# Moving columns of both layers' products taken in turn from two halves of the operand

## The chip, the cores and the metric

The kernel runs on 1 core of one Trainium2 chip. The metric is the device time of one execution in microseconds, as the median of several runs. One more execution is taken with a profiler; durations and rows below come from that one.

## The reference

Pooled attention feeds a two-layer block with a rational activation. Everything is float32. Cut to what matters:

```python
# q, k, v: (8, 8, 576, 64); pool = 8 keys or values are averaged into one
attn = softmax(q @ mean8(k).T / 8)            # 72 pooled keys per head
x = (attn @ mean8(v)) -> (4608, 512)          # tokens x (heads * head_dim)
h = x @ w_in                                  # (4608, 2048)
P = a[0] + a[1]*h + a[2]*h*h + a[3]*h*h*h
Q = 1 + abs(b[0])*abs(h) + abs(b[1])*h*h
out = (P / (Q + 1e-6)) @ w_out                # (4608, 512)
```

## The kernel before

**Blocks.** The 4608 tokens are worked in 18 blocks of 256 (`TOK`), the 2048 inner columns in 8 units of 256 (`NU`). For each block `attend` (line 860) makes the attention output, already transposed: 512 model columns on 4 x 128 partitions, 256 tokens along the free dimension. For each pair of block and unit there are three steps: `mm1` (line 925, first layer), `rational` (line 944, the activation on ScalarE, VectorE and GpSimd) and `mm2` (line 981, second layer).

**Split numbers.** The type fp32r keeps fewer bits of a float32. So each operand is kept as two fp32r parts, a high one and a low one, and each product is the sum of three: high by high, high by low, low by high. x is the pair of tiles `xs[0]`, `xs[1]` (128 x 4 x 256); a weight tile `w` has both parts, `w[:, 0, :]` and `w[:, 1, :]`.

**First layer.** `mm1` does 24 products for each block and unit into one PSUM bank `ph` (128 inner columns x 2 x 256 tokens). The stationary operand is 128 x 128 of `w_in`, the moving operand is `xs[xi][:, c, :]`: 256 consecutive tokens (line 938).

**Second layer.** `mm2` does 12 products for each block and unit into two banks `po` (128 tokens x 512 output columns, one for each half of the block). The stationary operand is 128 x 128 of the activation (`gh` or `gl`), the moving operand 512 consecutive columns of a row of `w_out` (line 991). The banks collect over the units; then `evict` (line 1024) scales and copies bank 0 on VectorE and bank 1 on ScalarE into `ob`, which is sent to `out`. Blocks 0 and 1 are done in two halves of the units: their first sum goes to memory and is fetched and added by `scalar_tensor_tensor` (line 1014).

**Where x is made.** `values` (line 826) multiplies the pooled values by the attention weights into a bank `pv` (2 x 256 tokens for two of the four groups of model columns), ScalarE copies it to `xs[0]` in fp32r (line 846) and VectorE subtracts that copy from `pv` into `xs[1]` (line 847). This happens twice in a block, for groups 0 and 1 and for groups 2 and 3.

**What sets the order.** Nothing is issued as it is written. Each operation is added to a `Plan` with a cost, a due time and what it reads and writes; `solve` (line 168) simulates the engines and picks the order of every engine, and `issue` (line 266, the calls on line 299) emits it. The costs are constants: 118.1 ns for a product of the first layer (line 935), 231.6 ns for one of the second (line 990). Between real products the plan puts filler products (line 290) where TensorE would stand idle: early ones multiply `identr` by itself with 256 moving columns, later ones add zeros, with one column of zeros repeated 256 times as the moving operand.

A dependency in the plan goes by `Lazy.box` (line 53): the region of a tile that an operand names. It is known only where the operand is cut by plain indices; with a `rearrange` it is empty, and an empty box meets every other one:

```python
            if name != "__getitem__":
                return ()
```

For the very first units of block 0, `mm1` splits its products into those of groups 0 and 1 and those of groups 2 and 3 (`parts`, line 930), so that the first can go ahead of the second half of x.

Of the kernel before, what the change touches and what calls it, by code (L numbers as in the profile page):

```python
# [8 lines left out]
F32 = mybir.dt.float32  # L9
# [3 lines left out]
ALU = mybir.AluOpType  # L13
# [9 lines left out]
class Lazy:  # L23
# [29 lines left out]
    def box(self):  # L53

        for name, args, _ in self.chain:
            if name == "bitcast":
                continue
            if name != "__getitem__":
                return ()
            idx = args[0] if isinstance(args[0], tuple) else (args[0],)  # L60
            out = []
            for i, n in zip(idx, self.tile.shape):
                out.append((i, i + 1) if isinstance(i, int) else
                           (i.start or 0, n if i.stop is None else i.stop))
            return tuple(out)
        return ()


def meet(a, b):
# [31 lines left out]
class Plan:  # L101
# [27 lines left out]
    def add(self, eng, cost, calls, port=False, claims=(), bytes=0, early=38, after=()):  # L129
# [5 lines left out]
        for _, args, kw in calls:  # L135
            every = list(args) + list(kw.values())
            dst = kw.get("out", args[0] if args else None)
            for v in every:
                if isinstance(v, Lazy) and v is not dst:
                    box = v.box()  # L140
                    op.deps.update(o for o, x in v.tile.writes if meet(x, box))
                    v.tile.reads.append((op, box))
                    touched[id(v.tile)] = v.tile
            if isinstance(dst, Lazy):
                t, box = dst.tile, dst.box()
                op.deps.update(o for o, x in t.writes if meet(x, box))
                op.deps.update(o for o, x in t.reads if meet(x, box))
                if box == ():
                    t.writes, t.reads = [], [r for r in t.reads if r[0] is op]
                t.writes.append((op, box))  # L150
                touched[id(t)] = t
# [167 lines left out]
def tile_pooled_attention_then_rational_moe(  # L319
# [18 lines left out]
    NT, DM = out.shape  # L338
    DFF = w_in.shape[1]
    P = 128  # L340
# [5 lines left out]
    TOK = 256  # L346
# [29 lines left out]
    def new(where, tag, shape, dtype, name):  # L376
        return plan.tile(*pools[where], shape, dtype, tag, name)

    def bank(name, shape):
        return new("ps", "ps", shape, F32, name)  # L380

    dve = Engine(plan, "dve", 0.09999999999999999, 1.04)
    act = Engine(plan, "act", 0.105, 0.85)
    gp = Engine(plan, "pool", 0.242, 2.021)

    def pe(ns, calls, claims=(), after=()):
        return plan.add("pe", ns / 1000, calls, claims=claims, after=after)

    def mm(out, lhsT, rhs, start, stop):
        return "matmul", (out,), dict(lhsT=lhsT, rhs=rhs, start=start, stop=stop)  # L390

    def dma(kbytes, dst, src, run=2048, issue=0.48, early=60.0, after=()):

        plan.add("sp", issue, [("dma_start", (dst, src), {})], early=early, after=after,
                 bytes=kbytes * 1024 * (1 + 312 / run))
# [52 lines left out]
    WS = 2.0 ** 8  # L448
# [220 lines left out]
    def segs(t0, n):  # L669

        r, t = [], t0
        while t < t0 + n:
            e = min(t0 + n, (t // S + 1) * S)
            r.append((t - t0, e - t0, t // S))
            t = e
        return r
# [149 lines left out]
    def values(i, hi, lo, before=None):  # L826

        xs = [new("xs", f"x{s}", [P, NJ, TOK], F32R, f"x{s}_{i}") for s in range(2)]
        for c in range(2):
            if before:  # L830
                before(c)
            pv = bank(f"pv{i}_{c}", [P, 2, TOK])
            calls = []
            for jj in range(2):
                j = 2 * c + jj
                for r0, r1, n in segs(i * TOK, TOK):
                    vh, vl = vm[n % 2]
                    o = pv[:, jj, r0:r1]
                    terms = ((o, vh[:, j, :], hi[:, j, r0:r1]), (o, vl[:, j, :], hi[:, j, r0:r1]),
                             (pv[:D, jj, r0:r1], vr[n % 2][:, j, :], lo[:, NJ + c, r0:r1]),  # L840
                             (o, vh[:, j, :], lo[:, j, r0:r1]))
                    calls += [mm(dst, vals, probs, s == 0, s == 3)
                              for s, (dst, vals, probs) in enumerate(terms)]
            pe(117.4 * 8 if len(calls) == 8 else 1635, calls, claims=xs)
            cs = slice(2 * c, 2 * c + 2)
            act(2 * TOK).copy(xs[0][:, cs, :], pv)
            dve(2 * TOK).tensor_tensor(
                out=xs[1][:, cs, :], in0=pv, in1=xs[0][:, cs, :].bitcast(F32),
                op=ALU.subtract)
        return xs  # L850

    prepared = set()
# [7 lines left out]
    def attend(i):  # L860
# [27 lines left out]
        if i >= SQ:  # L888

            for a in range(4):  # L890
# [15 lines left out]
            dve(2 * TOK, port=True).tensor_tensor(  # L906
                out=both[0], in0=both[1], in1=own, op=ALU.subtract)
        return values(i, hi, lo)


# [14 lines left out]
    def mm1(i, u, xs):  # L925
        ph = bank(f"ph{i}_{u}", [P, 2, TOK])
        n = DM // P
        w = weights["win", u]
        last = ()
        parts = [range(n)] if i or u > 1 else [range(n // 2), range(n // 2, n)]  # L930
        for h, cs in enumerate(parts):
            plan.now += 8 * h
            for f in range(2):
                for s, (wi, xi) in enumerate(((0, 0), (0, 1), (1, 0))):
                    last = pe(118.1 * len(cs), [
                        ("matmul", (ph[:, f, :],), dict(
                            lhsT=w[:, wi, (2 * c + f) * P:(2 * c + f + 1) * P],
                            rhs=xs[xi][:, c, :], start=f == 0 and s == 0 and c == 0,
                            stop=s == 2 and c == n - 1, skip_group_check=True))
                        for c in cs], after=last),  # L940
        plan.now -= 8 * h
        return ph
# [14 lines left out]
    def last(i, u):  # L957
        return i == NBLK - 1 and u == NU - 1
# [20 lines left out]
    pos, parts = {}, {}  # L979

    def mm2(i, u, gh, gl):
        u0, u1 = (0, NU) if i >= 2 else (0, NA) if u < NA else (NA, NU)
        if u == u0:
            pos[i] = [bank(f"po{i}_{u}_{m}", [P, DM]) for m in range(2)]
        w = weights["wout", u]
        terms = [(f, *x) for f in range(2) for x in ((gh, 0), (gh, 1), (gl, 0))]

        def products(n, ms):
            f, g, wi = terms[n]
            return pe(231.6 * len(ms), [  # L990
                mm(pos[i][m], g[:, f, m * P:(m + 1) * P], w[:, wi, f * DM:(f + 1) * DM],
                   u == u0 and n == 0, u == u1 - 1 and n == 5)
                for m in ms], claims=[pos[i][m] for m in ms])

        if last(i, u):
            for m in range(2):
                plan.now += 10.0 * m
                for n in range(6):
                    products(n, (m,))
                ob = new("dec", "m", [P, DM], F32, f"ob{i}_{m}")  # L1000
                evict(m, ob, pos[i][m])
                dma(256, out[i * TOK + m * P:i * TOK + (m + 1) * P, :], ob)
            return
        for n in range(6):
            end = products(n, (0, 1))
        if u < u1 - 1:
            return
        ob = new("dec", "m", [P, 2, DM], F32, f"ob{i}_{u}")
        if i < 2 and u0:
            dma(512, ob, parts.pop(i), after=(end,))  # L1010
        for m in range(2):
            po = pos[i][m]
            if i < 2 and u0:
                dve(DM).scalar_tensor_tensor(out=ob[:, m, :], in0=po, scalar=1.0 / WS,
                                             in1=ob[:, m, :], op0=ALU.mult, op1=ALU.add)
            else:
                evict(m, ob[:, m, :], po)
        if i < 2 and not u0:
            parts[i] = new("hbm", f"pd{i}", [P, 2, DM], F32, f"pd{i}")
            dma(512, parts[i], ob)  # L1020
        else:
            dma(512, out[i * TOK:(i + 1) * TOK, :].rearrange("(m p) x -> p m x", p=P), ob)

    def evict(m, dst, po):
        if m == 0:
            dve(DM).tensor_scalar(out=dst, in0=po, scalar1=1.0 / WS, scalar2=None, op0=ALU.mult)
        else:
            act(DM).activation(dst, po, AF.Copy, scale=1.0 / WS)
# [22 lines left out]
    xs, kept = {}, {}  # L1051
# [65 lines left out]
```

## Time and profile before

| | |
|---|---|
| median of 3 runs | 927.87 us (927.82 to 928.4) |
| the profiled execution's own time | 928.65 us |
| its span, from the first to the last instruction | 926.9 us |
| mean granted TensorE clock | 0.998 |
| busy: TensorE, VectorE, ScalarE, GpSimd | 99%, 82%, 73%, 57% of the span |

The profile's page lists the busy time of each engine, a chain of waits that is followed back from the last instruction, and groups of instructions. Nearly all instructions come from line 299, so groups are told apart by the names of their tiles. The length that a product has in such a row is the time it is in the pipeline, and consecutive products overlap; what a product costs in a stream is the time from its start to the next one's start. That is read from the chain or the timeline: the time of a stretch of one kind divided by its count, or the difference of two starts.

### The profile page before, as it was taken

How to read it: one execution, taken by the hardware profiler on the slowest of the kernel's cores; microseconds unless marked ns; L12 is line 12 of the kernel's file. 1: busy time of each engine (PE TensorE's matmuls, PEld its weight loads, DVE VectorE, ACT ScalarE, POOL GpSimd, SP SyncE). 2: the span in 40 equal slices, each digit the busy share in tenths (PEclk: the TensorE clock that was granted, in tenths of full speed). 3: DMA queues.
4: the chain of work that ended last, by engine and by line, in shares of the span. 5: the costliest groups of instructions: out<-in, count | busy, mean ns of one | idle time of the engine just before them, and what ended most of it. 6: DMA issues, size and time to landing. Idle time of an engine off the chain costs nothing.

```text
span 926.9 us, 17117 instructions
## 1 busy us (share of the span) xinstructions
PE 916.0 (99%) x6158; PEld 834.1 (90%) x6158; DVE 764.6 (82%) x1335; ACT 677.1 (73%) x1126; POOL 529.7 (57%) x474
## 2 busy tenths in 40 slices
PE   7999999999999999999999999999999999999998
PEld 7899999999998999999999899999999899999996
DVE  5989988798879888878888798879896988787764
ACT  2888888777677867776776877686867676777774
POOL 4787787685547644445644574457544755444452
PEclk9999999999999999999999999999999999999999
DMA  9995201163233412122603160215312231202000
GB/s 275 309 386 189 47 29 45 32 158 103 46 82 75 119 24 58 28 59 52 143 9 71 37 161 11 39 42 128 73 28 54 69 81 22 59 1 59 1 23 23
DMA packets 185072, 75.32 MB, mean 81 GB/s; under 512 B 162332, under 2 KB 162332, under 8 KB 184988
## 3 DMA queue, kind: packets, MB, share of 16 engines
q1 hardware_dynamic: 184988, 74.23, 31.1%
q8 instruction: 49, 0.80, 0.4%
q14 instruction: 35, 0.29, 0.1%
HBM read 50.59 MB, written 12.58 MB: 68 GB/s over the span
## 4 chain that ended last, share of the span: by engine, by line
PE 92%; DVE 2%; SPq 2%; ACT 1%; DMA 1%; issue 0%; POOL 0%; ACTq 0%
PE po L299 41%; PE ph L299 41%; PE pv L299 4%; PE ps L299 4%; SPq L299 2%; DMA q<-in_q_dram 1%; DVE t L299 1%; PE pvs L299 0%; PE pq L299 0%; DVE e L299 0%; DVE sm L299 0%; PE pk L299 0%; DVE am L299 0%; PE pm L299 0%; PE pvr L299 0%
## 5 line engine op out<-in xcount | busy, mean ns | idle before, releaser
L299 PEld LDWEIGHTS ph<-x,win 128*128 128x128 f32 x3264 | 480.1, 188 | 60.6 <-ACT x L299 0.9
L299 PE MATMUL ph<-x,win 128*128 128x256 f32 x3264 | 497.5, 279 | 0.8 <-ACT x L299 0.5
L299 PE MATMUL po<-wout,gh 128*128 128x512 f32 x1152 | 355.7, 395 | 0.0
L299 POOL TENSOR_TENSOR w<-w,r 128x512 f32<-128x512 f32 (+1 forms) x145 | 192.7, 1329 | 260.5 <-ACT r L299 257.4
L299 POOL TENSOR_TENSOR gl<-t,gh 128x512 fp32r<-128x512 f32 (+1 forms) x145 | 191.8, 1323 | 77.2 <-ACT gh L299 76.5
L299 PEld LDWEIGHTS po<-wout,gh 128*128 128x128 f32 x1152 | 179.7, 188 | 7.7 <-issue 0.4
L299 PE MATMUL po<-wout,gl 128*128 128x512 f32 x576 | 180.9, 395 | 0.0
L299 DVE SCALAR_TENSOR_TENSOR t<-t,abn,rp 128x512 f32<-128x512 f32 (+1 forms) x145 | 107.0, 739 | 50.2 <-ACT rp L299 48.5
L299 ACT ACTIVATE t<-ph,abn 128x512 f32<-128x512 f32 (+1 forms) x145 | 112.1, 773 | 34.9 <-PE ph L299 22.9
L299 DVE TENSOR_TENSOR t<-t,ph 128x512 f32<-128x512 f32 (+1 forms) x145 | 97.9, 676 | 37.4 <-ACT t L299 36.4
L299 ACT ACTIVATE r<-w,abn 128x512 f32<-128x512 f32 (+1 forms) x145 | 117.6, 811 | 13.4 <-POOL gl L299 6.8
L299 ACT ACTIVATE w<-ph 128x512 f32<-128x512 f32 (+1 forms) x145 | 86.1, 594 | 51.5 <-PE ph L299 31.2
L299 ACT CAST gh<-t 128x512 fp32r<-128x512 f32 (+1 forms) x145 | 88.8, 613 | 38.3 <-DVE t L299 37.0
L299 ACT ACTIVATE rp<-w 128x512 f32<-128x512 f32 (+1 forms) x145 | 86.6, 597 | 41.1 <-POOL w L299 39.5
L299 DVE SCALAR_TENSOR_TENSOR t<-t,abn,ph 128x512 f32<-128x512 f32 (+1 forms) x145 | 106.5, 735 | 2.4
L299 DVE SCALAR_TENSOR_TENSOR t<-rp,t 128x512 f32<-128x512 f32 (+1 forms) x145 | 98.5, 680 | 2.4
L299 DVE SCALAR_TENSOR_TENSOR rp<-w,rp 128x512 f32<-128x512 f32 (+1 forms) x145 | 98.8, 681 | 0.3
L299 PEld LDWEIGHTS po<-wout,gl 128*128 128x128 f32 x576 | 88.5, 188 | 2.2 <-issue 0.2
L299 ACT ACTIVATE rp<-rp 128x512 f32<-128x512 f32 (+1 forms) x145 | 84.2, 581 | 2.6
L299 POOL TENSOR_TENSOR e<-e,sm 128x576 f32<-128x576 f32 x36 | 42.0, 1184 | 22.0 <-DVE sm L299 16.1
L299 PE MATMUL pv<-am,vm 128*128 128x256 f32 (+3 forms) x288 | 45.0, 276 | 0.0
L299 PEld LDWEIGHTS pv<-am,vm 128*128 128x128 f32 x288 | 41.2, 189 | 0.3
(109 smaller groups left out, 850.2 us busy)
## 6 DMA issues: line engine op xcount, KB each, us to landing
am<-e SPq DMA_DIRECT2D x224, 48.0 KB, 2.1
out_dram<-ob SPq DMA_DIRECT2D x17, 512.0 KB, 3.2
rwin<-in_moe_w_in_dram SPq DMA_DIRECT2D x8, 1024.0 KB, 10.0
rwout<-in_moe_w_out_dram SPq DMA_DIRECT2D x8, 1024.0 KB, 10.8
st_k<-in_k_dram SPq DMA_DIRECT2D x12, 512.0 KB, 4.8
st_v<-in_v_dram SPq DMA_DIRECT2D x12, 512.0 KB, 4.0
q<-in_q_dram SPq DMA_DIRECT2D x144, 32.0 KB, 1.9
st_v<-in_v_dram SPq DMA_DIRECT2D x48, 64.0 KB, 2.2
```

The costliest lines, as they stand in the source:

```text
L299: getattr(engines[op.eng], name)(*map(value, args), **{k: value(v) for k, v in kw.items()})
```

## The change

Three views of a tile are added, which change only the order in which elements are visited. `woven` reads element 0 of the first half, element 0 of the second half, element 1 of the first half, and so on. Both layers' products take their moving operand through it. So that the results come out in their places, x is stored with the even tokens in its first half and the odd ones in its second (so the woven tokens are in order again), and the columns of `po`, which now alternate between the two halves of the output columns, are sorted when they are evicted. The cost constants of the plan stay.

```diff
+def woven(x):
+    return x.rearrange("p (a b) -> p b a", a=2)
+
+def sorted_out(x):
+    return x.rearrange("p (b a) -> p a b", a=2)
+
+def halves(x):
+    return x.rearrange("p (a b) -> p a b", a=2)
...
             cs = slice(2 * c, 2 * c + 2)
-            act(2 * TOK).copy(xs[0][:, cs, :], pv)
-            dve(2 * TOK).tensor_tensor(
-                out=xs[1][:, cs, :], in0=pv, in1=xs[0][:, cs, :].bitcast(F32),
-                op=ALU.subtract)
+            x, y = (z[:, cs, :].rearrange("p c (a b) -> p c a b", a=2) for z in xs)
+            sums = pv.rearrange("p c (b a) -> p c a b", a=2)
+            act(2 * TOK).copy(x, sums)
+            dve(2 * TOK).tensor_tensor(out=y, in0=sums, in1=x.bitcast(F32), op=ALU.subtract)
...
-                            rhs=xs[xi][:, c, :], start=f == 0 and s == 0 and c == 0,
+                            rhs=woven(xs[xi][:, c, :]), start=f == 0 and s == 0 and c == 0,
...
-                mm(pos[i][m], g[:, f, m * P:(m + 1) * P], w[:, wi, f * DM:(f + 1) * DM],
+                mm(pos[i][m], g[:, f, m * P:(m + 1) * P], woven(w[:, wi, f * DM:(f + 1) * DM]),
...
-                dve(DM).scalar_tensor_tensor(out=ob[:, m, :], in0=po, scalar=1.0 / WS,
-                                             in1=ob[:, m, :], op0=ALU.mult, op1=ALU.add)
+                to = halves(ob[:, m, :])
+                dve(DM).scalar_tensor_tensor(out=to, in0=sorted_out(po), scalar=1.0 / WS,
+                                             in1=to, op0=ALU.mult, op1=ALU.add)
...
     def evict(m, dst, po):
+        dst, po = halves(dst), sorted_out(po)
```

## Rows read from the trace of the kernel before

**Rows 1.** The page: span, busy time of each engine, clock in 40 slices.

```profile
span 926.9 us, 17117 instructions
PE 916.0 (99%) x6158; PEld 834.1 (90%) x6158; DVE 764.6 (82%) x1335; ACT 677.1 (73%) x1126; POOL 529.7 (57%) x474
PEclk9999999999999999999999999999999999999999
```

**Rows 2.** The page: the chain that ended last, by engine.

```profile
PE 92%; DVE 2%; SPq 2%; ACT 1%; DMA 1%; issue 0%; POOL 0%; ACTq 0%
```

**Rows 3.** Busy time by stretch: us, busy (instructions) of each engine, clock, DMA share, GB/s.

```profile
40.00:270.00 230.00, 229.22 (x1556) 208.21 (x1555) 200.63 (x334) 185.31 (x306) 163.47 (x123) 1.00 0.40 119
270.00:870.00 600.00, 599.75 (x4043) 546.98 (x4042) 503.11 (x893) 436.56 (x723) 321.24 (x271) 1.00 0.27 58
```

**Rows 4.** Groups of instructions by shape: products of both layers; busy us, mean ns, idle before.

```profile
L299 PE MATMUL ph<-x,win 128*128 128x256 f32 x3264 | 497.5, 279 | 0.8 <-ACT x L299 0.5 <-DVE x L299 0.3
...
L299 PE MATMUL po<-wout,gh 128*128 128x512 f32 x1152 | 355.7, 395 | 0.0
...
L299 PE MATMUL po<-wout,gl 128*128 128x512 f32 x576 | 180.9, 395 | 0.0
...
L299 PE MATMUL ph<-xr,win 128*128 128x256 f32 x192 | 28.6, 278 | 0.0
```

**Rows 5.** The chain in order of time: start us, us, what; long stretches and one cycle.

```profile
32.43 1.96 PE ps L299 x16
...
61.97 3.77 PE ph L299 x32
...
253.98 4.09 PE ph L299 x36
276.02 1.89 PE pv L299 x16
...
374.49 1.81 PE pv L299 x16
...
905.49 0.46 PE ph L299 x4
905.95 0.46 PE po L299 x2
...
911.01 12.14 PE po L299 x52
```

**Rows 6.** The timeline of TensorE around fillers: start us, us, what.

```profile
24.00 1.84 PE L290 MATMUL idle<-identr 128*128 128x256 f32 x14
25.68 0.27 PE L299 MATMUL pm<-identr,e 128*128 128x128 f32 x1
...
77.49 0.61 PE L290 MATMUL po<-zero,identr 128*128 128x256 f32 x4
77.93 0.38 PE L299 MATMUL pr<-identr,e 128*128 128x128 f32 x2
```

**Rows 7.** Groups by shape: copies out of PSUM, and two pairs of SBUF readers.

```profile
L299 DVE TENSOR_TENSOR x<-pv,x 128x512 fp32r<-128x512 f32 x36 | 24.8, 689 | 11.1 <-ACT x L299 10.5 <-PE pq L299 0.2
...
L299 ACT CAST x<-pv 128x512 fp32r<-128x512 f32 x36 | 21.1, 586 | 9.3 <-PE pv L299 9.2
...
L299 DVE TENSOR_SCALAR ob<-po 128x512 f32<-128x512 f32 x18 | 12.4, 690 | 19.6 <-PE po L299 19.5
...
L299 ACT ACTIVATE ob<-po 128x512 f32<-128x512 f32 x18 | 10.6, 590 | 9.3 <-PE po L299 9.2 <-POOL win L299 0.2
...
L299 ACT ACTIVATE m_win<-rwin 128x1024 f32<-128x1024 f32 x8 | 9.2, 1156 | 1.3 <-POOL win L299 1.0 <-POOL wout L299 0.4
...
L299 ACT CAST win<-m_win 128x1024 fp32r<-128x1024 f32 x8 | 8.4, 1052 | 1.1 <-DVE m_win L299 1.1
```

**Rows 8.** The chain around the first products of block 0: start us, us, what.

```profile
28.04 0.61 DVE x L299
...
28.68 0.76 PE ph L299 x4
29.45 0.94 PE pv L299 x8
30.39 0.44 PE pq L299 x4
30.82 1.18 PE ph L299 x8
```

## The prediction

> **What bounds the kernel now.** [...] The table by stretch shows where there is slack: from 40 to 870 us TensorE is free for about 1 us in all, while VectorE is busy 84 to 87% and ScalarE 73 to 81% [rows 3]. So the time is the sum of what the products cost, and a product's cost is the distance to the next start. How many there are is in the groups: 3264 + 192 = 3456 of the first layer with 256 moving columns, 1152 + 576 = 1728 of the second with 512 [rows 4].
>
> Now the distances, from stretches of one kind in the chain [rows 5]. First layer: 4.09 us / 36 = 113.6 ns in one stretch, 3.77 / 32 = 117.8 in another. Second layer, at the end: 12.14 / 52 = 233.5 ns. In most of the kernel four of the first alternate with two of the second, 0.46 us each, so 115 and 230 ns. [...] The filler with one column repeated takes (77.93 - 77.49) / 4 = 110 ns, the filler that reads 256 stored columns (25.68 - 24.00) / 14 = 120 ns [rows 6]: the same work for the array, only the read differs. And the attention's own product has two paces for one shape, 1.81 / 16 = 113 and 1.89 / 16 = 118 ns, in different blocks [rows 5]: the place of the operands matters.
>
> **The change, part by part.** No product, copy or DMA is added or removed. What changes is the order in which moving columns are read, and the order in which four kinds of copies read PSUM.
>
> Second layer. The trace has no product that reads columns alternately from two places. [...] That is (230 - 218) to (230 - 213) = 12 to 17 ns on each of 1728: 20.7 to 29.4 us saved.
>
> First layer. Its pace cannot fall as far: 36 in a row hold 113.6 ns, a stream with other data (pv) holds 113, and the repeated column 110 in a short run. I take 113.4 as a floor set by something other than the moving read, most likely the weight load that goes with each product. From a mean of about 115 to 116 (115 in the cycles, 117.8 in the slower stretches) that leaves some 1.5 ns on 3456, or 5 us saved; bounds nothing and 10 us; the upper cost bound, half pace, is 0.851 x 256 = 218 ns.
>
> Copies. x (36 on each engine) and `ob` (18 on each, and 4 sums) now read every second word of a bank. Nothing in the trace reads PSUM so. The nearest pair reads SBUF: ScalarE takes 1156 ns for every second of 2048 words against 1052 for 1024 in a row [rows 7], 10% more, part of it perhaps the function. Bounds: nothing, and double. At 10% it is 59 to 69 ns each. Doubled it would add 36 x 586 + 18 x 590 = 31.7 us to ScalarE and about 40 us to VectorE over the kernel, beside the path: the copies of a block's x are hidden by the products of the block before, and of TensorE's idle time only 0.8 us in all was spent waiting for x [rows 4]. If that cover were gone, one such delay of 0.06 us in 36 copies is 2 us. Only the last eviction stands uncovered at the end: 0.06 us, doubled 0.6. I take 0.1 us.
>
> The order in the plan. `woven` and the sorted views are made with `rearrange`, so their boxes are empty and meet everything. Three new dependencies follow. First, a product of `mm1` now waits in the plan for both halves of x. In block 0 the split of the first units loses its use: the 4 products at 28.68 us and, of the 8 at 30.82, those that need only the first half [rows 8] move behind the second half of x. They stood in a gap where TensorE had no other work, and later it has no gap. That is up to 14 products of 116 ns, 1.6 us lost; between nothing (a filler is displaced in their new place) and 2 us. I take 1.5. What waits behind them is the activation of the first unit, and no DMA. Second, high products of `mm2` wait for the low part of their weights, which is ready long before a unit's first second-layer product; price nothing, and at most one GpSimd subtraction in the first unit. Third, the second eviction of a block follows the first in the plan, 0.7 us later, with another bank free meanwhile; nothing. No queue's DMAs move, except as the whole plan shifts with these.
>
> What is late next: with TensorE some 3% faster, VectorE rises from 84 to about 87% of the middle stretch and ScalarE to 75%. Both still fit, but short waits for the activation chain can come. I give back 2 us for them; between nothing and 6.
>
> The sum, in the middle of the layer terms: -25 - 5 + 0.1 + 1.5 + 2 = -26.4, against the profiled execution's own 928.65 us: 902.2. That execution stands 0.8 us above the median of the runs shown, so **902** is my number for the median, give or take that. Full relief with nothing given back is 928.65 - 29.4 - 10 + 1 = 890; half relief with 6 given back is 920.
>
> **Rivals.** (a) Faster as above, 890 to 922.
>
> (b) The alternating read halves the pace of a stream. The place is the moving read of every product of both layers. [...] If fetching brings several neighbouring columns at once, a jump throws all but one away, and each column costs a fetch. It decides as soon as a fetch for one column takes longer than the weight-load floor leaves, 113.4 / 256 = 0.443 ns. [...]
>
> [...]
>
> (c) A milder loss: the jumps disturb the read as the places of operands do now. The filler that reads stored columns beside its own weight load has 120 ns, the slow pv blocks 118. With 120 for the first layer and 240 for the second everywhere: 3456 x 4 + 1728 x 10 = 31 us, so 960 us; a little less or more gives 932 to 990.
>
> [...]
>
> **How the numbers follow.** Chances: (a) 0.56, (b) 0.19, (c) 0.17, (d) 0.08. A difference of 0.2% or 1.9 us is about what a measurement of this kernel can tell from none. Faster by more: 0.56. Within: 0.08. Slower by more: 0.19 + 0.17 = 0.36. The range holds (a), (d) and (c): 890 to 985, 0.81. (b) is left out. The likeliest case's own range is 890 to 922.
>
> **What would show it.** Right: the stretch of second-layer products at the end falls from 233.5 to 213 to 220 ns, the cycle of four and two from 0.92 to about 0.89 us, long first-layer stretches all at 113 to 114, and the counts of the groups stay. The copies out of PSUM are 590 to 760 ns. The head shows the first `ph` products only after the second copy of x. Wrong: a pace of the last stretch near 430 ns is (b), near 240 (c), still 231 to 236 (d). If the pace falls and the time does not, TensorE has new idle time, and its releaser names the engine of the activation chain that became late.

## The result and the profile after

The changed kernel takes **907.22 us** (906.89 to 908.78, 4 runs) against 927.85 us of the kernel before in the same session; the ratio is 0.9782 with a 95% interval of 0.9765 to 0.9798. The forecast was 902 us in a range of 890 to 985, faster with a chance of 0.56. Its main rival, half the pace, did not come; two terms of its sum were far off and partly cancelled.

First the page of the changed kernel: span, busy time by engine, the chain by engine.

```profile
span 907.1 us, 17112 instructions
...
PE 887.9 (98%) x6158; PEld 826.4 (91%) x6158; DVE 763.7 (84%) x1335; ACT 677.3 (75%) x1126; POOL 525.0 (58%) x474
...
PE 51%; DVE 15%; ACT 9%; SPq 8%; POOL 5%; DMA 5%; issue 5%; DVEq 0%; ACTq 0%; POOLq 0%
```

The counts are those of [rows 1]. But the chain that was 92% TensorE [rows 2] is now 51%: the other engines have come into it. The long stretches of the chain (start us, us, what) show the products:

```profile
60.97 3.57 PE ph L314 x32
...
218.75 2.68 PE ph L314 x24
...
892.04 11.24 PE po L314 x52
```

Beside [rows 5]: the last stretch of the second layer went from 12.14 to 11.24 us, 233.5 to 216.2 ns for a product. The first layer's slow stretch went from 117.8 to 3.57 / 32 = 111.6 ns, and the one of 24 also has 111.7. The timeline of TensorE in the middle (start us, us, what):

```profile
340.33 0.61 PE L314 MATMUL ph<-x,win 128*128 128x256 f32 x4
340.78 0.60 PE L314 MATMUL po<-wout,gh 128*128 128x512 f32 x2
341.21 0.61 PE L314 MATMUL ph<-x,win 128*128 128x256 f32 x4
```

A cycle of four and two is 341.21 - 340.33 = 0.88 us where it was 0.92 [rows 5]. Both traces can be compared product by product, because the issue order is the same (below). The 3344 products of the first layer that stand at the usual distance from the next start in both (at most 122 ns) went from 383.8 to 371.6 us, and the 1668 of the second (at most 240 ns) from 385.8 to 361.8: 36 us saved. The time fell by 20.6 (19.9 between the two profiled executions), so some 16 us came back. Of these, 12.9 lie at 24 places where the next start is more than 0.15 us later than before. What TensorE waits for there, the table by stretch and its waits say (the table has the columns of [rows 3]; a wait has us in total, times, longest):

```profile
40.00:270.00 230.00, 227.81 (x1582) 209.39 (x1581) 203.02 (x336) 189.68 (x309) 162.00 (x123) 1.00 0.40 119
270.00:870.00 600.00, 591.90 (x4130) 553.48 (x4129) 510.41 (x907) 443.79 (x739) 326.41 (x278) 1.00 0.27 58
```

```profile
PE ph L314 <- ACT x L314: 4.2, 7, 1.0
...
PE ps L314 <- DVE qT L314: 2.0, 2, 1.2
PE ph L314 <- DVE x L314: 0.7, 2, 0.4
```

From 40 to 870 us TensorE was free for 1.0 us before [rows 3] and is free for 2.2 + 8.1 = 10.3 us now. It waits for the copies of x, 0.8 us before [rows 4] and 4.9 now, and for the transposed queries. One such place in the timeline:

```profile
705.05 0.61 PE L314 MATMUL ph<-x,win 128*128 128x256 f32 x4
705.50 0.60 PE L314 MATMUL po<-wout,gh 128*128 128x512 f32 x2
707.10 0.49 PE L314 MATMUL ph<-x,win 128*128 128x256 f32 x2 [1.00 <-ACT x L314]
708.15 0.49 PE L314 MATMUL ph<-x,win 128*128 128x256 f32 x2 [0.57 <-ACT x L314]
```

The first products of a block stand in front of its x. Two second-layer products that take 0.43 us are given 1.60 us.

The copies out of PSUM (groups by shape: busy us, mean ns, idle before) cost what they cost in [rows 7]:

```profile
L314 DVE TENSOR_TENSOR x<-pv,x 128x512 fp32r<-128x512 f32 x36 | 24.6, 686 | 6.4 <-ACT x L314 5.6 <-PE pq L314 0.2
...
L314 ACT CAST x<-pv 128x512 fp32r<-128x512 f32 x36 | 20.9, 580 | 3.7 <-PE pv L314 3.6
```

Apart from line numbers, the instructions of every engine are issued in the same order in both kernels. So the two traces differ by the pace of the products and by what followed from it, and by nothing that was planned otherwise.

### The profile page after: what moved, and what is told of

The parts are those of the page before. It is cut to its first block, busy times and chain, and to the rows that moved or that the text cites. A ratio compares the mean times of both kernels' runs of the same rounds, so it can differ in the third digit from the quotient of the medians.

```text
span 907.1 us, 17112 instructions
## 1 busy us (share of the span) xinstructions
PE 887.9 (98%) x6158; PEld 826.4 (91%) x6158; DVE 763.7 (84%) x1335; ACT 677.3 (75%) x1126; POOL 525.0 (58%) x474
## 4 chain that ended last, share of the span: by engine, by line
PE 51%; DVE 15%; ACT 9%; SPq 8%; POOL 5%; DMA 5%; issue 5%; DVEq 0%; ACTq 0%; POOLq 0%
PE ph L314 23%; PE po L314 23%; SPq L314 8%; DVE t L314 6%; ACT rp L314 3%; PE ps L314 3%; POOL gl L314 2%; DVE rp L314 2%; ACT gh L314 2%; PE pv L314 2%; POOL w L314 2%; DMA early<-in_v_dram 2%; DMA q<-in_q_dram 1%; ACT t L314 1%; DVE am L314 1%
## 5 line engine op out<-in xcount | busy, mean ns | idle before, releaser
L314 PEld LDWEIGHTS ph<-x,win 128*128 128x128 f32 x3264 | 473.8, 191 | 45.6 <-ACT x L314 6.5
L314 PE MATMUL ph<-x,win 128*128 128x256 f32 x3264 | 487.4, 276 | 5.2 <-ACT x L314 4.2
L314 PE MATMUL po<-wout,gh 128*128 128x512 f32 x1152 | 340.1, 382 | 0.4 <-ACT gh L314 0.4
L314 PE MATMUL po<-wout,gl 128*128 128x512 f32 x576 | 173.2, 382 | 0.0
L314 ACT ACTIVATE t<-ph,abn 128x512 f32<-128x512 f32 (+1 forms) x145 | 111.7, 771 | 25.0 <-PE ph L314 11.1
L314 PE MATMUL ps<-kpT,qT 128*128 128x144 f32 (+1 forms) x304 | 42.4, 294 | 2.9 <-DVE qT L314 2.0
```

Source lines behind the costliest of these rows:

```text
L314: getattr(engines[op.eng], name)(*map(value, args), **{k: value(v) for k, v in kw.items()})
```

## The experiments

**Each layer alone.** Theory A says that the alternation removes a stall of the moving read, product by product.

```diff
-                            rhs=woven(xs[xi][:, c, :]), ...
+                            rhs=xs[xi][:, c, :], ...
```

(with x stored in token order)

> Only the second layer takes its moving columns from two halves; x is stored in token order. Theory A (the alternation removes a stall of the moving read, product by product): the last stretch of 52 second-layer products has 216 to 218 ns each as in the changed kernel, the first layer stays at 113 to 115, and of the 24 us saved on 1728 products some third is given back in waits of TensorE: 908 to 914 us. Rival B (the gain is a gain of the whole stream, from the first layer's operand or its weight loads): the second layer stays above 225 ns and the time is above 920 us.

Measured: 914.69 us, ratio to before 0.9856 (0.9841 to 0.9871), a little over the expected range. The last stretch of 52 takes 11.24 us, 216 ns each. The first layer, expected unchanged, is not: in the cycles its four take 340.33 - 339.86 = 0.47 us in the timeline below, where before it was 0.46. Over the whole trace the mean of its usual distances (at most 122 ns) is 117.0 ns instead of 114.8, some 8 us more in all. The last line is the stretch at the end, from the chain.

```profile
339.86 0.63 PE L314 MATMUL ph<-x,win 128*128 128x256 f32 x4
340.33 0.59 PE L314 MATMUL po<-wout,gh 128*128 128x512 f32 x2
340.76 0.63 PE L314 MATMUL ph<-x,win 128*128 128x256 f32 x4
...
898.74 11.24 PE po L314 x52
```

The other way round:

```diff
-                mm(pos[i][m], ..., woven(w[:, wi, f * DM:(f + 1) * DM]), ...
+                mm(pos[i][m], ..., w[:, wi, f * DM:(f + 1) * DM], ...
```

(with evictions as before the change)

> Only the first layer takes its moving columns from two halves; x is stored even tokens first, the second layer and its evictions are as before the change. Theory A: first-layer products at 109 to 112 ns, second-layer products still 231 to 236; 12 us saved on 3456 products, a few given back: 917 to 923 us. Rival B: both layers become faster, 910 or less.

Measured: 921.16 us, ratio 0.9927 (0.991 to 0.9944). From the chain, a first-layer stretch and the last one of the second layer:

```profile
62.12 3.57 PE ph L314 x32
...
903.68 12.14 PE po L314 x52
```

The last stretch again takes 12.14 us, 233.5 ns each, while the first layer goes at 111 to 112. Each layer gains by its own operand, and rival B falls. The two gains in time, 13.0 and 6.6 us, add up to 19.6 of the 20.6 us.

**The copies alone.** Both products read columns in a row, the copies stay sorted, so tokens and output columns come out in another order.

> The copies out of PSUM are sorted as in the changed kernel, all products read columns in a row; tokens and output columns come out in another order. Theory A: the copies cost nothing (686 and 580 ns each as in both kernels), so the time of the kernel before, 926 to 930 us. Rival C (reading every second word of PSUM costs something that the products' gain hid): slower than before by over 3 us, or copies over 700 and 600 ns.

Measured: 927.89 us, ratio 1.0003 (0.9994 to 1.0012). The copies of x take 688 and 586 ns, as in [rows 7]. Reading every second word of PSUM costs nothing that these runs can tell; rival C falls.

**What gave 16 us back?** The plan still has 118.1 and 231.6 ns as the cost of a product. Theory D: its order is made for slower products. Rival E: VectorE and ScalarE cannot feed a faster TensorE.

```diff
-                    last = pe(118.1 * len(cs), [
+                    last = pe(111.5 * len(cs), [
...
-            return pe(231.6 * len(ms), [
+            return pe(217.0 * len(ms), [
```

> The changed kernel with the plan's cost of a product set to what the profile of the changed kernel shows: 111.5 ns in the first layer and 217.0 in the second, where it had 118.1 and 231.6. Theory D (the 16 us that TensorE gave back in waits come from an order that was planned for slower products): waits of TensorE fall to the 10 us they had before the change, 892 to 899 us. Rival E (they come from VectorE and ScalarE, which cannot keep up with a faster TensorE whatever the order): 903 to 909 us, waits as in the changed kernel.

Measured: 908.73 us, ratio 0.9791 (0.9777 to 0.9806): no gain over the changed kernel. The total alone would have settled for rival E, but the stretches tell otherwise. From 270 to 870 us TensorE was busy 597.3 of 600 us, where the changed kernel had 591.9. What was lost lies at the start (table by stretch, columns as in [rows 3]):

```profile
40.00:50.00 10.00, 8.36 (x35) 6.85 (x36) 8.65 (x15) 6.44 (x17) 4.09 (x6) 0.66 1.11 337
...
270.00:870.00 600.00, 597.30 (x4185) 560.78 (x4184) 515.22 (x912) 451.06 (x747) 329.83 (x280) 1.00 0.27 58
```

From 40 to 50 us TensorE did 35 products, after short transposes with waits between them, and its granted clock averaged 0.66; the changed kernel did 70 products there at 1.00. The first second-layer product started at 58.9 us, 5.9 us later than in the changed kernel. Also, where the new plan expects TensorE to stand idle it fills in products: 60 of the zero fillers instead of 14. So the next trial kept the old costs, and with them the old start, for the first eight pairs of block and unit:

```diff
-                    last = pe(118.1 * len(cs), [
+                    last = pe((118.1 if i < 2 and u < NA else 111.5) * len(cs), [
...
-            return pe(231.6 * len(ms), [
+            return pe((231.6 if i < 2 and u < NA else 217.0) * len(ms), [
```

> The changed kernel with the new costs of a product (111.5 and 217.0 ns) only outside the first eight pairs of block and unit; those keep 118.1 and 231.6, and with them the order of the start. Theory D2 (with the new costs the steady part gains 8 us, and what the first trial lost is the start, where its second-layer products stood 8 us behind and the clock fell): the steady gain stays, the start is as in the changed kernel, 897 to 902 us. Rival E (the waits come from VectorE and ScalarE, whatever the order): 905 to 909 us.

Measured: **901.45 us** (900.72 to 902.78), ratio 0.9718 (0.9697 to 0.9739): faster than both kernels. Its table by stretch:

```profile
40.00:270.00 230.00, 226.76 (x1591) 209.99 (x1590) 202.14 (x334) 189.02 (x308) 161.54 (x123) 1.00 0.41 120
270.00:870.00 600.00, 598.70 (x4206) 563.18 (x4206) 526.83 (x918) 453.08 (x751) 330.03 (x280) 1.00 0.27 59
```

From 270 us on TensorE is free for 1.3 us instead of 8.1; before that still for 3.2, and 54 zero fillers take the place of some other waits (17 of them, 1.9 us, after 270 us). So in the total the order is the cause of about 6 of the 16 us; theory D holds for these. What remains was tried once more with nearer due times:

```diff
-    HEAD, PACE, SLOW, SLOWS = 15.5, 6.2, 5, 2 * NA
+    HEAD, PACE, SLOW, SLOWS = 15.5, 5.9, 5, 2 * NA
```

> As the kernel with new costs after the start, with the plan's due times 5.9 us apart instead of 6.2. Theory D (what is left of the waits is order): 896 to 900 us. Rival E (VectorE and ScalarE cannot feed TensorE any faster): 900 to 903 us, as without it.

Measured: 900.82 us, ratio 0.9708 (0.9692 to 0.9724), which cannot be told from the run before it; theory D's range is missed and rival E's is met.

The totals mix two parts, and the starts of the products tell them apart. The first is up to the start of the 385th of the 1728 second-layer products, when the first four blocks are done; the second is from there to the end (us):

| | before | changed | new costs | late new costs | nearer due times |
|---|---|---|---|---|---|
| first four blocks | 257.9 | 254.4 | 261.8 | 256.6 | 257.1 |
| the rest | 669.0 | 652.7 | 645.0 | 643.5 | 642.1 |

Of the 36 us, 28 are saved in products of the second part, where the changed kernel gains 16.3 us and so gives 12 back. With the new costs it gains 24.0 to 26.9 and gives back only 1 to 4. There the order was the cause, and VectorE and ScalarE do feed the faster products: rival E falls for this part. In the first four blocks the products save 8 us, but none of the three runs with new costs gains more than 1.3 us there, so most of the 10 us that are still given back (36 saved in products, 26 to 27 in time) lie in them. Whether order or the limit of another engine or of the DMAs holds them stays open.

**Which orders of columns are fast?** One kernel, an order for each block. Line 338 is the line of the calls here.

```diff
+PATTERNS = {
+    4: ("p (a b) -> p a b", dict(a=2)),
+    5: ("p (a b) -> p b a", dict(a=2)),
+    6: ("p (b a) -> p a b", dict(a=2)),
...
+    12: ("p (x a b) -> p x b a", dict(a=2, b=4)),
...
-                mm(pos[i][m], ..., woven(w[:, wi, f * DM:(f + 1) * DM]), ...
+                mm(pos[i][m], ..., in_order(i, w[:, wi, f * DM:(f + 1) * DM]), ...
```

> As the changed kernel, but each of the blocks 4 to 16 reads the moving columns of the second layer in an order of its own, so that output columns come out in other places: 4 in a row; 5 two halves in turn; 6 every second, then the rest; 7 every fourth; 8 every sixteenth; 9 two halves in turn, two columns each; 10 four each; 11 sixteen each; 12 two neighbouring groups of 4 columns (16 bytes) in turn; 13 two neighbouring groups of 16 in turn; 14 four quarters in turn; 15 sixteen places in turn; 16 neighbours swapped within groups of 4. Fast is 216 to 218 ns, slow 229 to 236. Theory A1 (a group of 16 bytes stalls when it gives two columns one after the other): fast where neighbours in the order lie in different groups, blocks 5, 7, 8, 12, 13, 14, 15; slow in 4, 6, 9, 10, 11. Theory A2 (it takes two places far apart): fast in 5, 14, 15 and perhaps 9 to 11, slow in the rest. [...]

Measured: 1015.52 us in a single run. From the timeline of TensorE, a pair of second-layer products and the start after it, in blocks 4, 5, 6, 7, 9 and 12:

```profile
262.24 0.63 PE L338 MATMUL po<-wout,gh 128*128 128x512 f32 x2
262.70 0.61 PE L338 MATMUL ph<-x,win 128*128 128x256 f32 x4
...
312.38 0.60 PE L338 MATMUL po<-wout,gl 128*128 128x512 f32 x2
312.81 0.61 PE L338 MATMUL ph<-x,win 128*128 128x256 f32 x4
...
362.29 1.07 PE L338 MATMUL po<-wout,gh 128*128 128x512 f32 x2
363.18 0.62 PE L338 MATMUL ph<-x,win 128*128 128x256 f32 x4
...
432.56 1.08 PE L338 MATMUL po<-wout,gl 128*128 128x512 f32 x2
433.46 0.63 PE L338 MATMUL ph<-x,win 128*128 128x256 f32 x4
...
562.80 0.82 PE L338 MATMUL po<-wout,gh 128*128 128x512 f32 x2
563.45 0.61 PE L338 MATMUL ph<-x,win 128*128 128x256 f32 x4
...
720.21 0.60 PE L338 MATMUL po<-wout,gl 128*128 128x512 f32 x2
720.64 0.61 PE L338 MATMUL ph<-x,win 128*128 128x256 f32 x4
```

Half of each difference is the pace of one product: 230 ns in a row, 215 with two halves in turn, 445 for every second column, 450 for every fourth, 325 for two columns from each half, and 215 for two neighbouring groups of four in turn. The other blocks, by the middle of their start distances: every sixteenth 431; four from each half 250, sixteen from each 241; neighbouring groups of sixteen in turn 216; four quarters 276; sixteen places 433; neighbours swapped within groups of four 233, as in a row.

Both theories fall. A1 wants every second and every fourth column apart: block 7 alternates groups with each column and has 450 ns, about half the pace of a row. A2 wants far places: block 12 takes neighbours 16 bytes apart and is as fast as the halves, 215 ns.

What fits best is to look at every other column of the order by itself (theory P in the expectation below). In a row, columns 0, 2 then 4, 6: two of one way lie in one group of four (230 ns). Halves, or neighbouring groups in turn: four (215). Swapped neighbours (0, 2, 1, 3): two, as in a row (233). Every second column (0, 2, 4, 6): one way sees 0, 4, 8, one to a group (445). Not all blocks follow: in 10 and 11 each way takes two running columns from a group, as in a row, and they cost 250 and 241 ns; block 9 and the quarters lie in between, at 325 and 276. The first layer was run with the same orders:

```diff
-                            rhs=woven(xs[xi][:, c, :]), ...
+                            rhs=in_order(i, xs[xi][:, c, :]), ...
```

> As the changed kernel, but each of the blocks 4 to 16 reads the moving tokens of the first layer in the same orders as in the run before by block number (256 columns here), so that tokens come out in other places; the second layer takes its columns from two halves everywhere. Theory A1: 109 to 112 ns in blocks 5, 7, 8, 12, 13, 14, 15, and 114 to 118 in 4, 6, 9, 10, 11. Theory A2: 109 to 112 only in 5, 14, 15.

Measured: 1012.79 us in a single run. Block 6 in the timeline, a stretch of twelve and the start after it:

```profile
360.94 2.92 PE L338 MATMUL ph<-x,win 128*128 128x256 f32 x12
363.66 0.63 PE L338 MATMUL po<-wout,gh 128*128 128x512 f32 x2
```

By the middle of the distances, in ns: 117 in a row, 112 with halves, 228 for every second, 233 for every fourth, 220 for every sixteenth, 166, 126 and 120 for two, four and sixteen from each half, 112 for neighbouring groups of four or sixteen in turn, 143 for quarters, 220 for sixteen places, 117 swapped. It is nearly the same ranking with half the columns, and against A1 and A2 in the same blocks.

**A test of theory P with orders it had not seen.**

```diff
+    5: ("p (a b c) -> p c b a", dict(a=2, c=2)),
+    6: ("p (a b c) -> p c b a", dict(a=2, c=4)),
+    7: ("p (x a b) -> p x b a", dict(a=4, b=4)),
+    8: ("p (x a b) -> p x b a", dict(a=2, b=8)),
+    11: ("each twice", 1),
...
+    15: ("one", 512),
```

> As the changed kernel, with further orders of the second layer's moving columns by block; output columns come out in other places, block 11 uses only the first 256 columns, and block 15 one column for all (one token in the first layer too), so those leave work out. Block 4: a row; 5: two halves in turn, in each every second column, then the rest; 6: two halves in turn, in each every fourth; 7: four neighbouring groups of 4 columns in turn; 8: two neighbouring groups of 8 in turn; 11: each column twice running; 12: two neighbouring groups of 4 in turn; 13: two halves in turn; 15: one column repeated. Theory P, made from the run before (every other column of the order goes one way and the rest another; each way keeps up if four of its columns running lie in one group of 16 bytes, loses 8% if two do, and takes two cycles for a column if each is in a new group): 231 to 234 ns in block 4, the same in 5, 430 to 460 in 6, 270 to 295 in 7, 216 to 218 in 8, 11, 12, 13. Rival T (it takes two places in turn, however the columns lie in each): 216 in 5 and 6 too. Rival L (it is the columns taken from a group before it is left for good: 4 in turn with another are fast, 2 or 1 are half pace): 430 to 460 in 5. If the floor of 216 ns and of 112 in the first layer has nothing to do with reading, block 15 shows the same 216 and 112.

Measured: 942.68 us in a single run. Blocks 5, 6, 7, 11 and 15 in the timeline:

```profile
312.34 0.63 PE L338 MATMUL po<-wout,gl 128*128 128x512 f32 x2
312.80 0.61 PE L338 MATMUL ph<-x,win 128*128 128x256 f32 x4
...
362.00 1.07 PE L338 MATMUL po<-wout,gh 128*128 128x512 f32 x2
362.89 0.62 PE L338 MATMUL ph<-x,win 128*128 128x256 f32 x4
...
433.03 0.70 PE L338 MATMUL po<-wout,gl 128*128 128x512 f32 x2
433.57 0.61 PE L338 MATMUL ph<-x,win 128*128 128x256 f32 x4
...
626.01 0.60 PE L338 MATMUL po<-wout,gl 128*128 128x512 f32 x2
626.44 0.61 PE L338 MATMUL ph<-x,win 128*128 128x256 f32 x4
...
822.93 0.60 PE L338 MATMUL po<-wout,gl 128*128 128x512 f32 x2
823.37 0.61 PE L338 MATMUL ph<-x,win 128*128 128x256 f32 x4
```

Two halves in turn with every second column: 230 ns, the pace of a row. So it is not the two places (rival T wanted 216), nor the two columns taken from a group before it is left (rival L wanted 430). Every fourth in each: 445. Four neighbouring groups in turn: 270, a hair under the range. Each column twice running: 215, though neighbours come from the same group. Blocks 8, 12 and 13 have 216. In block 15, where one column is repeated, the second layer has 220 and the first 111 to 112: the floor of both is there even when the read never changes its column.

## Why the prediction was right or wrong

**What bounds the kernel**: right for the kernel before. Only the pace of the products was touched, and the time followed it, but by 20.6 of the 36 us. One reading of the working is off: the filler with 120 ns reads the 128 columns of `identr` twice over, not 256 stored ones; only the price of rival (c) leans on it.

**Second layer** (12 to 17 ns each, 20.7 to 29.4 us): right in size. It is 17.3 ns in the last stretch and 14 on average, 24 us in all against a term of 25. No run shows the 213 and 218 ns from which this term is worked out: the last stretch has 216.2 ns, the fastest orders have 215 to 216, and one column repeated has 220. Nor is it the two places that count: two halves with every second column in each have 230 ns, the pace of a row, and neighbours 16 bytes apart have 215, as halves do. In nearly all the orders tried, the pace goes by how many of every other column lie running in one group of four.

**First layer** (floor 113.4, 5 us): mis-sized. The floor was read from stretches that were themselves slowed by the read; alternating halves reach 111.6 in a stretch and 109 right after a second-layer product, and 12 us were saved. That there is a floor which the order of the read does not set is right (block 15: 111 to 112 ns with one column repeated); that it is the weight load was not tested.

**Copies** (0.1 us): right; the copies alone gave a ratio of 1.0003.

**The order in the plan** (1.5 us lost at the start): wrong, by misreading `Lazy.box`. It returns at the first plain index of the chain and never looks at a `rearrange` behind it; only a `rearrange` that comes first empties the box. The account of `box` in the section on the kernel before, that any `rearrange` empties it, is wrong in the same way. The issue order is the same in both kernels, and the first `ph` products still follow the first copy of x, at 27.72 us, ahead of the second half.

**What is late next** (2 us, bound 6): mis-sized most, and the bound was too low: of 36 us, 16 came back. The share of busy time of VectorE and ScalarE said that both would fit; what it could not say is that an order laid out to the tenth of a microsecond for slower products places TensorE's next block right behind its x. After the first four blocks 12 us came back, and 8 to 11 of these went away in the runs whose plan was told the new costs.

So -25 - 5 + 4 was forecast, -24 - 12 + 16 came. That the total lies only 5 us from the forecast is in part luck: the first layer gained 7 us more than its term, and that paid for over half of the 12 us by which the waits were underrated.

**Rivals.** Half the pace (b): its price is real, but for another order of columns. The 0.851 ns for a column that stands for half pace is that of the plain float32 scores, 1.96 us for 16 products [rows 5] of 144 columns each, and makes 436 ns for 512; block 6 has 445. Halves in turn have four running columns of each way in a group, and a product has 216 ns where a row has 233. (c), 240 ns, and (d), no difference, are excluded by 216 ns.

## What to carry to other kernels

When TensorE is the bound, compare the distance of product starts under several orders of the moving columns. For fp32r operands in a row it was 233.5 ns here with 512 columns and 117.8 with 256, and taking the columns in turn from two places, each read in a row, made it 216.2 and 111.6; steps of two, four or sixteen in a single place made it 445, 450 and 431 with 512 columns and 228, 233 and 220 with 256. After that, measure the stretches and not the total: here 16 of the 36 us saved in products came back, and after the start most of that was kept once the order behind it was laid out anew.

## What was not expected of the hardware

- The pace of an fp32r moving read follows every other column: 216 ns for 512 with four of them running in a group of four columns, 230 to 233 with two (241 and 250 where the order also changes its place after 16 or 4 columns), 431 to 450 with one. How the chip does this inside is not shown.
- Some orders lie in between: a way that alternates between two groups of which it takes four columns each costs 270 (four neighbouring groups) or 276 (quarters), two each 325, all of them less than the 431 to 450 of one column to a group. What keeps them from the slow pace is not shown.
- Reading every second word of PSUM cost VectorE and ScalarE nothing that shows: 686 and 580 ns for 512 elements, 689 and 586 in a row.
- With only the second layer faster, the first became slower, 117.0 ns on average instead of 114.8 and 0.47 us instead of 0.46 for its four in a cycle; why was not tried.
